# Channel part, first product: seven half products for a pair of row blocks and a pair of hidden tiles, with the prepared weights kept in DRAM

## The chip, the cores and the metric

The kernel runs on one core of a Trainium2 chip. Its engines are PE (matrix products), DVE (vector), ACT (activations), POOL and SP, which issues the DMAs here; each works through its own list in order and waits for the others at semaphores. The metric is the device time of one execution in microseconds (us); less is better. Before the change it is 751.38 us, the median of three runs (751.0 to 753.13).

## What is computed

The attention (local and pooled, 4 x 8 heads, 576 rows of 64) gives `x`, 4 x 576 x 512. Then come a gated layer and a mixing layer, cut to what matters:

```python
h = np.maximum(x @ w_in, 0.0)                       # 512 -> 1024
conv = sum over k of cw[k] * h shifted by k - 1     # three taps along the rows
x = h * sigmoid(conv) @ w_out                       # 1024 -> 512
u = x + (x.T @ U @ V).T                             # rank 32, along the rows
ch = np.maximum(u @ w_ch1, 0.0) @ w_ch2             # 512 -> 2048 -> 512
return u + ch
```

The last two lines are the channel part. The change concerns `u @ w_ch1`.

## The kernel before

The 2304 rows of all four batches are cut into six blocks `g` of 384 rows (`TB`), each of three chunks `c` of 128. Every large product is made of float32 numbers split in two parts, a rounded one ("hi", made by ACT) and the rest ("lo", made by DVE or POOL); three passes (hi by hi, hi by lo, lo by hi) give the product, so each tile of it costs three matmuls.

The order of all work is written out by hand in one long string, `SEQ`. Each of its words names a function and its arguments, and the instructions of each engine stand in the order of these words. A scheduler moves nothing. The string runs through the attention pairs with the unpacking of the weights beside them, through the gated layer (`g1` L647 and `g2` L701), the mixing layer (`mix_in`, `mix_out`) and the channel part, with the stages overlapping.

The weights arrive as 64-bit floats, 512 KB a tile of 128 x 512 (`w_load`). They are unpacked in four steps: one on ACT (L511), three on DVE (L513, L515, L518). Then `w_hi` (ACT, L531) and `w_lo` (POOL or DVE, L534) split them. There are 16 tiles of the gated layer and 32 of the channel part: `w_ch1` at the even, `w_ch2` at the odd places. Before the change all 32 are split once and stay in SBUF.

The channel part runs over the blocks `g` (6) and the hidden tiles `f` of 128 columns (16), that is 96 units `m`:

- `ut_trans` (L759), `ut_hi` (L763), `ut_lo` (L767): per block, four transposed tiles of `u`, split.
- `g3` (L775): 4 chunks of 128 x 3 passes = 12 matmuls of 384 columns into one PSUM bank. Two banks `g` take turns.
- `relu3_hi` (ACT, L780) and `relu3_lo` (DVE, L784): clip and split, straight from the bank into a tile `a` (two tiles take turns).
- `g4` (L793): 3 chunks x 3 passes = 9 matmuls of 512 columns into the three accumulators of the block.
- `flush4` (L801): adds the sum to `u` and writes the rows out, once per chunk.

Of the kernel before, what the change touches and what calls it, by code (L numbers as in the profile page):

```python
# [180 lines left out]

P = 128
NQ, NW = 24, 32
NAW2 = 6
# [711 lines left out]
```

## Time and profile before

| | |
|---|---|
| median of three runs | 751.38 us |
| profiled execution, its own time | 748.79 us |
| its span, first to last instruction | 746.8 us |
| PE busy | 730.4 us, 98% |
| DVE, ACT, POOL busy | 387.8, 295.0, 170.4 us |
| mean granted clock of PE | 0.979 |

The profiled execution lies 2.6 us under the median. An engine's share is an average over stages: the first 100 us are the only stretch in which PE has gaps; from then on it is busy without one. DVE is close to full in the first 120 us and nearly full from 300 to 400 us, where the weights of the channel part are unpacked, and almost idle after that.

### The profile page before, as it was taken

What the parts mean: (1) busy time and instruction counts of PE and PEld (TensorE: products, weight loads), DVE (VectorE), ACT (ScalarE), POOL (GpSimd) and SP (SyncE); (2) the same over time, 40 slices, a digit from 0 to 9 for tenths busy, and PEclk for the clock granted to TensorE, in tenths of its full rate; (3) what the DMA queues carried; (4) which work ended last, traced back from release to release, by engine and by line L of the source; (5) the groups of instructions that cost most, each with busy time, mean ns of one, the idle gap of its engine ahead of it and who ended that gap; (6) DMA issues with size and microseconds to landing.
All of it is one profiled execution on the core that took longest, in us unless ns stands there. A gap on an engine that the chain in (4) does not pass through costs nothing.

```text
span 746.8 us, 15411 instructions
## 1 busy us (share of the span) xinstructions
PE 730.4 (98%) x6655; PEld 651.0 (87%) x6655; DVE 387.8 (52%) x649; ACT 295.0 (39%) x667; POOL 170.4 (23%) x160
## 2 busy tenths in 40 slices
PE   8789999999999999999999999999999999999998
PEld 5578798988888989988998999998989989999887
DVE  6989998867565887889985111311131131112112
ACT  4558676656465856675543111211111111111111
POOL 3765645423233643353330000000000000000000
PEclk9569999999999999999999999999999999999999
DMA  8887523312013000561501000100010010001001
GB/s 243 277 281 240 195 75 90 99 37 72 25 58 113 1 1 29 181 222 51 226 28 43 1 0 1 43 1 0 1 43 1 0 43 1 1 0 43 1 1 42
DMA packets 16387, 52.42 MB, mean 70 GB/s; under 512 B 1984, under 2 KB 2496, under 8 KB 16320
## 3 DMA queue, kind: packets, MB, share of 16 engines
q1 hardware_dynamic: 16320, 51.44, 20.7%
q8 instruction: 52, 0.85, 0.5%
q14 instruction: 15, 0.12, 0.0%
HBM read 46.72 MB, written 4.72 MB: 69 GB/s over the span
## 4 chain that ended last, share of the span: by engine, by line
PE 91%; DMA 5%; DVE 2%; ACT 0%; issue 0%; DVEq 0%; SPq 0%
PE g L775 27%; PE acc L793 26%; PE g L647 14%; PE acc L701 13%; PE O L454 3%; DMA raw<-in_w_dram 2%; PE S L340 1%; DMA vw<-in_vw_dram 1%; PE h L725 1%; PE Sd L393 1%; PE ut L759 1%; PE O L462 1%; PE Td L434 1%; DMA vr<-in_vr_dram 1%; DMA qk<-in_qk_dram 1%; PE mx L746 1%
## 5 line engine op out<-in xcount | busy, mean ns | idle before, releaser
L775 PE MATMUL g<-uT,w 128*128 128x384 f32 x1152 | 213.6, 338 | 0.0
L793 PE MATMUL acc<-w,a 128*128 128x512 f32 x864 | 207.7, 392 | 0.0
L775 PEld LDWEIGHTS g<-uT,w 128*128 128x128 f32 x1152 | 202.3, 188 | 5.1 <-DVE a L784 0.7
L784 DVE SCALAR_TENSOR_TENSOR a<-g,a 128x384 fp32r<-128x384 f32 x96 | 53.4, 556 | 265.7 <-ACT a L780 265.4
L793 PEld LDWEIGHTS acc<-w,a 128*128 128x128 f32 x864 | 161.2, 188 | 31.5 <-issue 0.4
L780 ACT ACTIVATE a<-g 128x384 fp32r<-128x384 f32 x96 | 47.1, 491 | 281.4 <-PE g L775 152.8
L647 PE MATMUL g<-xhl,w 128*128 128x386 f32 (+1 forms) x576 | 117.9, 347 | 0.0
L701 PE MATMUL acc<-w,ghl 128*128 128x512 f32 x432 | 110.0, 396 | 0.0
L647 PEld LDWEIGHTS g<-xhl,w 128*128 128x128 f32 x576 | 102.4, 191 | 5.3 <-issue 1.4
L701 PEld LDWEIGHTS acc<-w,ghl 128*128 128x128 f32 x432 | 79.3, 188 | 14.9 <-issue 0.6
L674 DVE SCALAR_TENSOR_TENSOR g<-h,cw,g 128x384 f32<-128x384 f32 x96 | 59.4, 619 | 22.3 <-ACT g L669 20.5
L534 POOL TENSOR_TENSOR w<-wval,w 128x512 fp32r<-128x512 f32 x34 | 47.5, 1397 | 73.1 <-ACT w L531 71.2
L693 POOL TENSOR_TENSOR ghl<-ct,ghl 128x384 fp32r<-128x384 f32 x40 | 44.0, 1099 | 85.5 <-ACT ghl L690 84.9
L515 DVE SCALAR_TENSOR_TENSOR wval<-raw,wval 128x512 uint32<-128x512 uint32 x48 | 40.5, 846 | 0.9
L531 ACT ACTIVATE w<-wval 128x512 fp32r<-128x512 f32 x48 | 30.0, 628 | 23.3 <-DVE wval L518 23.1
L518 DVE SCALAR_TENSOR_TENSOR wval<-raw,wval 128x512 uint32<-128x512 uint32 x48 | 36.3, 765 | 0.8
L653 ACT ACTIVATE h<-g 128x386 f32<-128x386 f32 (+1 forms) x48 | 23.6, 491 | 27.1 <-PE g L647 26.8
L511 ACT ACTIVATE wval<-raw 128x512 f32<-128x512 f32 x48 | 31.2, 668 | 7.5 <-DMA raw<-in_w_dram 4.1
L454 PEld LDWEIGHTS O<-PT,vw 32*64 32x64 f32 x1536 | 26.3, 144 | 8.8 <-issue 4.7
L454 PE MATMUL O<-PT,vw 32*64 32x24 f32 x1536 | 28.1, 220 | 4.6 <-ACT PT L439 2.3
L678 ACT ACTIVATE g<-g 128x384 f32<-128x384 f32 x48 | 22.7, 474 | 14.6 <-DVE g L674 14.4
L669 ACT ACTIVATE g<-h,cw 128x384 f32<-128x384 f32 x48 | 28.0, 583 | 1.1
(97 smaller groups left out, 639.7 us busy)
## 6 DMA issues: line engine op xcount, KB each, us to landing
raw<-in_w_dram SPq DMA_DIRECT2D x48, 512.0 KB, 4.8
qk<-in_qk_dram SPq DMA_DIRECT2D x16, 576.0 KB, 4.3
vw<-in_vw_dram SPq DMA_DIRECT2D x16, 384.0 KB
vr<-in_vr_dram SPq DMA_DIRECT2D x16, 288.0 KB
out_dram<-u SPq DMA_DIRECT2D x17, 256.0 KB, 2.0
uvr<-in_v_dram SPq DMA_DIRECT2D x1, 576.0 KB
uvr<-in_u_dram SPq DMA_DIRECT2D x1, 320.0 KB
out_dram<-u SPq DMA_DIRECT2D x2, 128.0 KB
```

Of the source, the lines that this page charges most:

```text
L454: nc.tensor.matmul(o[D * h:D * h + D, jh, c:c + NQ], e["vw"][32 * s:32 * s + 32, t, a], e["PT"][32 * s:32 * s + 32, t, 32 * a:32 * a + NQ] ...
L515: nc.vector.scalar_tensor_tensor(out=d, in0=lo, scalar=29, in1=d, op0=ALU.logical_shift_right, op1=ALU.bitwise_or)
L518: nc.vector.scalar_tensor_tensor(out=d, in0=hi, scalar=0x80000000, in1=d, op0=ALU.bitwise_and, op1=ALU.bitwise_or)
L534: eng.tensor_tensor(W[k][:, 1], vals.pop(k), W[k][:, 0].bitcast(F32), op=ALU.subtract)
L647: nc.tensor.matmul(gp[n][:, :wd], w[:, a, cc], xhl[g, cc][:, b, :wd], start=cc == 0 and i == 0, stop=cc == NCC - 1 and i == 2)
L674: nc.vector.scalar_tensor_tensor(out=o, in0=inner(g, hts[n], k), scalar=cw[:, k * NF + f:k * NF + f + 1], in1=o, op0=ALU.mult, op1=ALU.add)
L693: eng.tensor_tensor(ghl[n][:, 1], cts.pop(n), ghl[n][:, 0].bitcast(F32), op=ALU.subtract)
L701: nc.tensor.matmul(acc[g][c], t[:, a, c * P:(c + 1) * P], w[:, b], start=f == 0 and i == 0, stop=f == NF - 1 and i == 2)
L775: nc.tensor.matmul(gp["3", m][:, :TB], w[:, a, cc], uT[g, cc][:, b, :TB], start=cc == 0 and i == 0, stop=cc == NCC - 1 and i == 2)
L780: nc.scalar.activation(out=t[:, 0], in_=gp["3", m][:, :TB], func=AF.Relu)
L784: nc.vector.scalar_tensor_tensor(out=t[:, 1], in0=gp.pop(("3", m))[:, :TB], scalar=0.0, in1=t[:, 0].bitcast(F32), op0=ALU.max, op1=ALU.sub ...
L793: nc.tensor.matmul(acc2[g][c], t[:, a, c * P:(c + 1) * P], w[:, b], start=f == 0 and i == 0, stop=f == NF2 - 1 and i == 2)
```

## The change

`u @ w_ch1` is now computed for a pair of row blocks (`r`, three pairs) and a pair of hidden tiles (`f`, eight pairs) at once. With the 512 columns of `u` cut in two halves, this is a 2 x 2 by 2 x 2 product of half-size pieces, and Strassen's scheme (in Winograd's form) makes it from seven products of sums instead of eight products. A half product is 2 chunks x 3 passes = 6 matmuls, so a unit `q` = (r, f) takes 7 x 6 = 42 matmuls where four units of before, its equal in work, took 48.

What comes with it:

- **Sums of weights.** `s_add` makes four sums of 128 x 256 pieces per `f`; `s_hi`, `s_lo` split the seven factors into tiles `as` (ten in turn, `NAS`). For `r` = 0 they are made, used and written to DRAM (`s_write`, 256 KB each, 56 in all); for `r` = 1 and 2 they are read back (`s_read`, 112 in all). The `w_ch2` tiles stay in SBUF as before, one per pair of places (`w_home`).
- **Sums of u.** Per pair of blocks there are eight groups of three transposes, as before (`u_trans`); then `v_copy` (ACT) and `v_sub` (DVE) make the sums, `b_hi` and `b_lo` split 14 tiles. For `r` = 0 the transposes use the banks `mx0`, `mx1`; for `r` = 1 and 2 they use the two banks of the products.
- **Products.** `product(r, f, j)` runs six matmuls. Products 0, 2, 4, 5 go one on top of the other into the first bank, 1 and then 3, 6 into the second. Between them ACT copies the partial sum out of the first bank (`p_copy`, three per unit) and DVE adds the second bank to such a copy (`p_add`, three per unit). `relu3_hi`, `relu3_lo` and `g4` then work for four results: three from the copies in SBUF, one from the bank.
- **Accumulators.** Two blocks are open at once, so six banks hold them; `mtile` gives three of these to the mixing layer before.
- **The list.** The whole `SEQ` string is new, the attention and the gated layer included. `WAY`, the KB that may be under way behind a load before the next one starts, is 900 instead of 600.

```diff
-    KPB = 3
-    WAY, NLIM = 600, 44
+    KPB, NAS = 3, 10
+    WAY, NLIM = 900, 44
...
+    def s_write(f, j):
+        nc.sync.dma_start(store[f][j], As[0, f, j].rearrange("p a x -> p (a x)").bitcast(F32))
...
+    def v_copy(r, k, i):
+        if i == 0:
+            vb[r, k] = [pools["pm"].tile([P, 2, 512], F32, name="vb", tag="x2a")]
+        nc.scalar.activation(out=vb[r, k][0][:, i, :TB], in_=ut[r, k, i][:, :TB], func=AF.Copy)
...
+    def product(r, f, j):
+        q = r * NFP + f
+        if j in (0, 1, 3):
+            bank[q, int(j > 0)] = gtile(int(j > 0))
+        o = bank[q, int(j in (1, 3, 6))][:, :TB]
+        w = As[r, f, j].rearrange("p a (c j) -> p a c j", c=HC)
+        n = 0
+        for k in range(HC):
+            for a, b in ((0, 0), (0, 1), (1, 0)):
+                nc.tensor.matmul(o, w[:, a, k], Bs[r, j, k][:, b, :TB], start=j in (0, 1, 3) and n == 0, stop=n == 3 * HC - 1, skip_group_check=True)
+                n += 1
+
+    def p_copy(q, i):
+        t = tp[q, i] = ph.tile([P, XW], F32, name="tp", tag="h", bufs=3)
+        nc.scalar.activation(out=t[:, :TB], in_=bank[q, 0][:, :TB], func=AF.Copy)
+
+    def p_add(q, i):
+        t = tp[q, (0, 2, 1)[i]][:, :TB]
+        nc.vector.tensor_tensor(t, bank[q, 1][:, :TB], t, op=ALU.add)
...
-    def g3(m, cc):
...
```

On PE, late in the channel part, where the list of before alternates long runs of `g3` (L775) and `g4` (L793):

```order
L775 MATMUL g<-uT,w 128x384 x15
L793 MATMUL acc<-w,a 128x512 x18
L775 MATMUL g<-uT,w 128x384 x24
L793 MATMUL acc<-w,a 128x512 x18
L775 MATMUL g<-uT,w 128x384 x48
L793 MATMUL acc<-w,a 128x512 x36
```

and the same place now, in unit 18 and at the start of unit 19 (L883 is `product`, L915 `g4`):

```order
L883 MATMUL g<-bt,as 128x384 x6
L915 MATMUL acc<-w,a 128x512 x6
L883 MATMUL g<-bt,as 128x384 x6
L915 MATMUL acc<-w,a 128x512 x3
L883 MATMUL g<-bt,as 128x384 x6
L915 MATMUL acc<-w,a 128x512 x18
L883 MATMUL g<-bt,as 128x384 x18
```

The runs are shorter: one product or a few between groups of `g4`, because each copy out of a bank has to be over before the next product on that bank.

On DVE, in the stage that unpacks the channel weights, before (L513, L515, L518 unpack, L784 is the lower part of the clipped tile, L534 that of a weight):

```order
L784 SCALAR_TENSOR_TENSOR a<-g,a 128x384
L513 TENSOR_SCALAR wval<-wval 128x512
L515 SCALAR_TENSOR_TENSOR wval<-raw,wval 128x512
L518 SCALAR_TENSOR_TENSOR wval<-raw,wval 128x512
L784 SCALAR_TENSOR_TENSOR a<-g,a 128x384
L518 SCALAR_TENSOR_TENSOR wval<-raw,wval 128x512
L534 TENSOR_TENSOR w<-wval,w 128x512 x2
```

and now (L543, L545, L548 unpack; L892 is `p_add`, L903 `relu3_lo`, L805 `s_add`, L821 `s_lo`):

```order
L805 TENSOR_TENSOR sv<-wval 128x256
L892 TENSOR_TENSOR tp<-g,tp 128x384
L548 SCALAR_TENSOR_TENSOR wval<-raw,wval 128x512
L903 SCALAR_TENSOR_TENSOR a<-tp,a 128x384
L903 SCALAR_TENSOR_TENSOR a<-g,a 128x384
L821 TENSOR_TENSOR as<-wval,as 128x256
L892 TENSOR_TENSOR tp<-g,tp 128x384
L821 TENSOR_TENSOR as<-wval,as 128x256
L821 TENSOR_TENSOR as<-sv,as 128x256 x4
```

Additions that PE waits for (L892, L903) now stand among the unpacking and the splitting of the sums.

On PE, where the transposes of the last rows of `u` stand, before:

```order
L775 MATMUL g<-uT,w 128x384 x24
L759 MATMUL ut<-ident,u_4779 128x128 x6
L793 MATMUL acc<-w,a 128x512 x18
L775 MATMUL g<-uT,w 128x384 x3
L759 MATMUL ut<-ident,u_4779 128x128 x3
L775 MATMUL g<-uT,w 128x384 x45
```

and now, between the second and the third pair of blocks (L836 transposes):

```order
L836 MATMUL g<-ident,u_4494 128x128 x3
L836 MATMUL g<-ident,u_4889 128x128 x3
L915 MATMUL acc<-w,a 128x512 x6
L836 MATMUL g<-ident,u_4889 128x128 x3
L915 MATMUL acc<-w,a 128x512 x9
L836 MATMUL g<-ident,u_4494 128x128 x6
L836 MATMUL g<-ident,u_4889 128x128 x6
L915 MATMUL acc<-w,a 128x512 x3
L836 MATMUL g<-ident,u_4494 128x128 x3
L915 MATMUL acc<-w,a 128x512 x6
L883 MATMUL g<-bt,as 128x384 x30
```

All eight groups of transposes of a pair now stand together, in the banks that the products use, with 24 matmuls of `g4` among them and no product.

## Rows read from the trace of the kernel before

**Rows 1.** Page: busy time, share, instructions; the span in 40 slices, tenths busy.

```profile
PE 730.4 (98%) x6655; PEld 651.0 (87%) x6655; DVE 387.8 (52%) x649; ACT 295.0 (39%) x667; POOL 170.4 (23%) x160
...
PE   8789999999999999999999999999999999999998
...
DVE  6989998867565887889985111311131131112112
...
PEclk9569999999999999999999999999999999999999
```

**Rows 2.** Chain of work that ended last: start us, us, engine, tile, line, matmuls.

```profile
660.00 8.16 PE acc L793 x36
...
726.52 8.39 PE g L775 x48
```

**Rows 3.** Groups by line and form: busy us, mean ns, idle before and its releaser.

```profile
L775 PE MATMUL g<-uT,w 128*128 128x384 f32 x1152 | 213.6, 338 | 0.0
L793 PE MATMUL acc<-w,a 128*128 128x512 f32 x864 | 207.7, 392 | 0.0
...
L784 DVE SCALAR_TENSOR_TENSOR a<-g,a 128x384 fp32r<-128x384 f32 x96 | 53.4, 556 | 265.7 <-ACT a L780 265.4
L780 ACT ACTIVATE a<-g 128x384 fp32r<-128x384 f32 x96 | 47.1, 491 | 281.4 <-PE g L775 152.8 <-PE acc L793 128.5
...
L801 DVE TENSOR_TENSOR u<-u,acc 128x256 f32<-128x256 f32 x2 | 0.8, 418 | 0.0
```

**Rows 4.** Timeline at 592 us, one tight handoff: start, us, engine, line; [idle before].

```profile
592.10 3.58 PE L793 MATMUL acc<-w,a 128*128 128x512 f32 x15
594.36 0.49 ACT L780 ACTIVATE a<-g 128x384 fp32r<-128x384 f32 x1 [5.76 <-PE acc L793]
594.88 0.56 DVE L784 SCALAR_TENSOR_TENSOR a<-g,a 128x384 fp32r<-128x384 f32 x1 [5.70 <-ACT a L780]
595.49 2.06 PEld L775 LDWEIGHTS g<-uT,w 128*128 128x128 f32 x12 [0.24 <-DVE a L784]
595.52 2.36 PE L775 MATMUL g<-uT,w 128*128 128x384 f32 x12
```

**Rows 5.** Windows of 20 us: PE, PEld, DVE, ACT, POOL busy, clock, DMA share, GB/s.

```profile
340.00:360.00 20.00, 20.00 (x101) 17.92 (x100) 18.40 (x33) 9.27 (x17) 4.98 (x4) 1.00 0.08 27
360.00:380.00 20.00, 20.00 (x108) 17.98 (x107) 17.86 (x32) 11.78 (x22) 7.57 (x7) 1.00 0.62 237
```

**Rows 6.** DVE and POOL from 340 to 400 us by line and form, columns as in rows 3.

```profile
L515 DVE SCALAR_TENSOR_TENSOR wval<-raw,wval 128x512 uint32<-128x512 uint32 x19 | 14.3, 758 | 0.5
L518 DVE SCALAR_TENSOR_TENSOR wval<-raw,wval 128x512 uint32<-128x512 uint32 x20 | 13.7, 695 | 0.4
L513 DVE TENSOR_SCALAR wval<-wval 128x512 uint32<-128x512 uint32 x19 | 8.7, 466 | 0.2 <-ACT wval L511 0.2
...
L534 POOL TENSOR_TENSOR w<-wval,w 128x512 fp32r<-128x512 f32 x13 | 18.3, 1410 | 42.3 <-ACT w L531 42.3
```

**Rows 7.** Single lines over the span: min/median/max ns, first and last start.

```profile
L513 DVE TENSOR_SCALAR wval<-wval x48: 411/420/1519, 18.3 to 395.3; 128x512 uint32<-128x512 uint32 x48
...
L515 DVE SCALAR_TENSOR_TENSOR wval<-raw,wval x48: 644/692/2355, 19.5 to 395.8; 128x512 uint32<-128x512 uint32 x48
...
L534 POOL TENSOR_TENSOR w<-wval,w x34: 1254/1298/1765, 22.8 to 398.0; 128x512 fp32r<-128x512 f32 x34
...
L420 POOL TENSOR_TENSOR vd<-vr x12: 721/736/1054, 8.3 to 212.9; 72x256 f32<-72x256 f32 x12
```

**Rows 8.** Timeline at 337 us, a POOL instruction and the DVE instruction beside it.

```profile
337.43 1.30 POOL L716 TENSOR_TENSOR x<-u,x 128x512 fp32r<-128x512 f32 x1 [0.67 <-ACT x L712]
...
337.53 1.74 DVE L515 SCALAR_TENSOR_TENSOR wval<-raw,wval 128x512 uint32<-128x512 uint32 x1
```

**Rows 9.** DMA issues of the whole span, KB each, median us from issue to landing.

```profile
raw<-in_w_dram SPq DMA_DIRECT2D x48, 512.0 KB, 4.8
...
out_dram<-u SPq DMA_DIRECT2D x17, 256.0 KB, 2.0
```

More of the change, by code (lines that the diff above doesn't have):

```diff
@@ L215, in mixer_kernel @@
     pv = ctx.enter_context(tc.tile_pool(name="pv", bufs=3, side="right", reuse_waits="tile"))
-    ph = tc.alloc_tile_pool(name="ph", bufs=1, side="right", reuse_waits="tile")
+    ph = ctx.enter_context(tc.tile_pool(name="ph", bufs=1, side="right", reuse_waits="tile"))
+    pe = ctx.enter_context(tc.tile_pool(name="pe", bufs=1, side="right", reuse_waits="tile"))
     px = tc.alloc_tile_pool(name="px", bufs=1, side="right", reuse_waits="tile")
-    pe = tc.alloc_tile_pool(name="pe", bufs=1, side="right", reuse_waits="tile")
+    dram = ctx.enter_context(tc.tile_pool(name="dram", bufs=1, space=bass.MemoryType.DRAM))
     pa = tc.alloc_tile_pool(name="pa", bufs=1, reuse_waits="tile")
@@ L491, in w_home @@
         g, i = k
[L492 to L494 removed]
+        return wp, f"w{i if g == 1 else i // 2}"
     def w_load(*k):
@@ L722, in mix_in @@
         if j == 4 * odd:
-            hps[b] = pools["psb"].tile([P, DM], F32, name="h1", tag="hh")
+            hps[b] = mtile(2, "h1")
         for a in range(2):
@@ L738, in mix_out @@
     def mix_out(pair, j):
-        p = mx[pair, j] = pools["psb"].tile([P, DM], F32, name="mx", tag="mx", bufs=2)
+        p = mx[pair, j] = mtile((pair * KPB * NCH + j) % 2, "mx")
         mm = []
@@ L751, in mix_add, with half @@
         nc.vector.tensor_tensor(u, u, mx.pop((pair, j)), op=ALU.add)
-    uT, acc2, a_, ut = {}, {}, {}, {}
-    def ut_trans(g, cc):
-        p = ut[g, cc] = pools["psb"].tile([P, 512], F32, name="ut", tag="mx", bufs=2)
+    NFP = NF2 // 2
+    As, Bs, vb, ut, a_, acc2, sv, tp, bank = {}, {}, {}, {}, {}, {}, {}, {}, {}
+    HC = NCC // 2
+    store = [[dram.tile([P, 512], F32, name=f"s{f}_{j}") for j in range(7)] for f in range(NFP)]
+    def half(i, k):
+        return vals[2, i][:, 256 * k:256 * k + 256]
@@ new lines, in s_add, with s_src @@
+    def s_add(eng, f, i):
+        w, x = 4 * f, 4 * f + 2
+        if i == 0:
+            sv[f] = pools["wa"].tile([P, 4, 256], F32, name="sv", tag="sv")
+            a, b = half(x, 0), half(x, 1)
+        elif i == 1:
+            a, b = sv[f][:, 0], half(w, 0)
+        elif i == 2:
+            a, b = half(w, 0), half(x, 0)
+        else:
+            a, b = half(w, 1), sv[f][:, 1]
+        eng.tensor_tensor(sv[f][:, i], a, b, op=ALU.subtract if i else ALU.add)
+    def s_src(f, j):
+        if j < 2 or j == 5:
+            return half(4 * f + 2 * (j == 5), int(j > 0))
+        return sv[f][:, {2: 1, 3: 0, 4: 2, 6: 3}[j]]
@@ new lines, in s_tile, with s_hi, s_lo, s_read @@
+    def s_tile():
+        return pools["wa"].tile([P, 2, 256], F32R, name="as", tag="as", bufs=NAS)
+    def s_hi(f, j):
+        As[0, f, j] = s_tile()
+        nc.scalar.activation(out=As[0, f, j][:, 0], in_=s_src(f, j), func=AF.Copy)
+    def s_lo(eng, f, j):
+        t = As[0, f, j]
+        eng.tensor_tensor(t[:, 1], s_src(f, j), t[:, 0].bitcast(F32), op=ALU.subtract)
+    def s_write(f, j):
+        nc.sync.dma_start(store[f][j], As[0, f, j].rearrange("p a x -> p (a x)").bitcast(F32))
+    def s_read(r, f, j):
+        t = As[r, f, j] = s_tile()
+        nc.sync.dma_start(t.rearrange("p a x -> p (a x)").bitcast(F32), store[f][j])
@@ L758, in ut_trans, with u_trans @@
+    def u_trans(r, i):
+        k, i = divmod(i, 4)
+        g, cc = ((2 * r, k), (2 * r + 1, k), (2 * r + 1, k + HC), (2 * r, k + HC))[i]
+        p = ut[r, k, i] = (mtile if r == 0 else gtile_named)(i % 2, "ut")
         for c in range(NCH):
             nc.tensor.transpose(p[:, c * P:(c + 1) * P], U_[g][:, c, cc * P:(cc + 1) * P], ident)
-    def ut_hi(g, cc):
-        t = uT[g, cc] = xt.tile([P, 2, XW], F32R, name="uT", tag="xt")
-        nc.scalar.activation(out=t[:, 0, :TB], in_=ut[g, cc][:, :TB], func=AF.Copy)
@@ L765, in ut_lo @@
-    def ut_lo(g, cc):
-        t = uT[g, cc]
-        nc.vector.tensor_tensor(t[:, 1, :TB], ut.pop((g, cc))[:, :TB], t[:, 0, :TB].bitcast(F32), op=ALU.subtract)
-    def g3(m, cc):
-        g, f = divmod(m, NF2)
-        if cc == 0:
-            gp["3", m] = gtile()
-        w = W[2, 2 * f].rearrange("p a (c j) -> p a c j", c=NCC)
-        for i, (a, b) in enumerate(((0, 0), (0, 1), (1, 0))):
-            nc.tensor.matmul(gp["3", m][:, :TB], w[:, a, cc], uT[g, cc][:, b, :TB],
-                             start=cc == 0 and i == 0, stop=cc == NCC - 1 and i == 2)
@@ L778, in relu3_hi, with gtile_named @@
-    def relu3_hi(m):
-        t = a_[m] = p1.tile([P, 2, TB], F32R, name="a", tag="ga")
-        nc.scalar.activation(out=t[:, 0], in_=gp["3", m][:, :TB], func=AF.Relu)
-    def relu3_lo(m):
-        t = a_[m]
-        nc.vector.scalar_tensor_tensor(out=t[:, 1], in0=gp.pop(("3", m))[:, :TB], scalar=0.0, in1=t[:, 0].bitcast(F32),
-                                       op0=ALU.max, op1=ALU.subtract)
-    def g4(m, c):
-        g, f = divmod(m, NF2)
-        if f == 0:
-            acc2.setdefault(g, {})[c] = pools["psg"].tile([P, DM], F32, name="acc", tag=f"acc{c}")
-        t, w = a_[m], W[2, 2 * f + 1]
+    def gtile_named(k, name):
+        return gtile(k)
@@ new lines, in v_copy, with v_sub @@
+    def v_copy(r, k, i):
+        if i == 0:
+            vb[r, k] = [pools["pm"].tile([P, 2, 512], F32, name="vb", tag="x2a")]
+        nc.scalar.activation(out=vb[r, k][0][:, i, :TB], in_=ut[r, k, i][:, :TB], func=AF.Copy)
+    def v_sub(r, k, i):
+        if i == 1:
+            vb[r, k].append(pools["pm"].tile([P, 2, 512], F32, name="vb", tag="x2b"))
+        (a, s), (b, o) = (((0, 0), (0, 0)), ((0, 0), (1, 0)), ((0, 1), (0, 1)), ((1, 0), (1, 1)))[i]
+        nc.vector.tensor_tensor(vb[r, k][b][:, o, :TB], ut[r, k, (1, 2, 2, 3)[i]][:, :TB], vb[r, k][a][:, s, :TB], op=ALU.subtract)
@@ new lines, in b_src, with b_hi @@
+    def b_src(r, k, j):
+        if j in (0, 1, 6):
+            return ut[r, k, {0: 0, 1: 3, 6: 2}[j]][:, :TB]
+        a, s = {2: (1, 0), 3: (0, 0), 4: (0, 1), 5: (1, 1)}[j]
+        return vb[r, k][a][:, s, :TB]
+    def b_hi(r, k, j):
+        i = 2 * j + k
+        if i < 6:
+            t = pools["pb"].tile([P, 2, TB], F32R, name="bt", tag=f"b{i}")
+        elif i == 6:
+            t = pools["wa"].tile([P, 2, TB], F32R, name="bt", tag="b6")
+        else:
+            t = xt.tile([P, 2, XW], F32R, name="bt", tag="xt")
+        Bs[r, j, k] = t
+        nc.scalar.activation(out=t[:, 0, :TB], in_=b_src(r, k, j), func=AF.Copy)
@@ new lines, in p_copy, with r_src, relu3_hi @@
+    def p_copy(q, i):
[4 more added lines that the diff above has]
+        nc.vector.tensor_tensor(t, bank[q, 1][:, :TB], t, op=ALU.add)
+    def r_src(q, k):
+        return bank[q, 0][:, :TB] if k == 3 else tp[q, (0, 2, 1)[k]][:, :TB]
+    def relu3_hi(q, k):
+        t = a_[q, k] = p1.tile([P, 2, TB], F32R, name="a", tag="ga")
+        nc.scalar.activation(out=t[:, 0], in_=r_src(q, k), func=AF.Relu)
@@ new lines, in relu3_lo, with g4 @@
+    def relu3_lo(q, k):
+        t = a_[q, k]
+        nc.vector.scalar_tensor_tensor(out=t[:, 1], in0=r_src(q, k), scalar=0.0, in1=t[:, 0].bitcast(F32),
+                                       op0=ALU.max, op1=ALU.subtract)
+    def g4(q, n, c):
+        k, blk, fo = ((0, 0, 0), (1, 1, 1), (3, 0, 1), (2, 1, 0))[n]
+        r, f = divmod(q, NFP)
+        g = 2 * r + blk
+        if f == 0 and n < 2:
+            acc2.setdefault(g, {})[c] = mtile(c, "acc") if blk else pools["psg"].tile([P, DM], F32, name="acc", tag=f"acc{c}")
+        t, w = a_[q, k], W[2, 2 * (2 * f + fo) + 1]
@@ L792, in g4 @@
         for i, (a, b) in enumerate(((0, 0), (0, 1), (1, 0))):
             nc.tensor.matmul(acc2[g][c], t[:, a, c * P:(c + 1) * P], w[:, b],
-                             start=f == 0 and i == 0, stop=f == NF2 - 1 and i == 2)
+                             start=f == 0 and n < 2 and i == 0, stop=f == NFP - 1 and n >= 2 and i == 2)
     def flush4(g, c):
@@ L825, in mixer_kernel @@
         "mi": mix_in, "mH": mix_h, "mo": mix_out, "ma": mix_add,
-        "u": ut_trans, "uT": ut_hi, "uL": ut_lo, "3": g3, "r3": relu3_hi, "R3": relu3_lo, "4": g4, "o": flush4,
+        "sa": lambda *k: s_add(GP, *k), "sA": lambda *k: s_add(DV, *k), "sh": s_hi, "sl": lambda *k: s_lo(DV, *k),
+        "sL": lambda *k: s_lo(GP, *k), "sw": s_write, "sr": s_read, "u": u_trans, "bv": v_copy, "bt": v_sub, "bh": b_hi,
+        "bl": lambda *k: b_lo(DV, *k), "bL": lambda *k: b_lo(GP, *k), "p": product, "pc": p_copy, "pa": p_add,
+        "rh": relu3_hi, "rl": relu3_lo, "4": g4, "o": flush4,
     }
```

30 lines of the change are left out of this document (14 added, 16 removed), and 354 rows, old and new, of the table SEQ.

## The prediction, made before the changed kernel was run

> **What bounds the kernel now.** I read the page first. PE is busy for 98% of the span, in its row of 40 slices only the first three and the last are under nine tenths, and its granted clock is down in the second and third alone [rows 1]. So the kernel is bound by the number and width of its matmuls, and anything that leaves matmuls out is worth their whole time, as long as PE finds its operands ready. What a matmul costs is read from the chain, where long runs stand in order of time: 48 of `g3` take 8.39 us, 0.175 us each, and 36 of `g4` take 8.16 us, 0.227 us each [rows 2]. (The means of 338 and 392 ns [rows 3] overlap and aren't used.) Short runs cost no more than long ones there. Then I read DVE, since what the change adds lies there: it is 92% and 89% busy in the two windows in which the weights are unpacked, and PE is full in both all the same [rows 5].
>
> **What is removed.** A pair of blocks and of hidden tiles takes 42 matmuls instead of 48, in 24 units: 144 matmuls fewer. 144 x 0.175 = 25.2 us off PE, all of it from the stretch in which PE is full. `g4` keeps its 864, the transposes their number.
>
> **The copies and additions between products.** Each of the 24 units adds three copies (ACT) and three additions (DVE) of 128 x 384, 0.49 and 0.56 us each by the nearest rows, `relu3_hi` and `relu3_lo` [rows 3]. After the first pair of blocks ACT and DVE have little else to do: 7 such ACT instructions are 3.4 us, 7 DVE ones 3.9 us, beside a unit of 42 x 0.175 + 36 x 0.227 = 15.5 us. It is not their sum that counts but whether each ends in time. For that I take one tight handoff of before apart [rows 4]: the run of 15 starts at 592.10, so its ninth matmul, which frees the tile `a`, ends near 592.10 + 9 x 0.227 = 594.14. ACT starts at 594.36, 0.22 later; DVE ends at 595.44; PE loads weights again at 595.49. So ACT and DVE together need about 1.35 us, one of them alone 0.22 + 0.49 (0.56) + 0.05 = 0.76 (0.83). There, six matmuls of `g4`, 1.36 us, lay in between, and PE lost some 0.02 us. In the new list I counted the matmuls in each gap. Where one copy or addition has to be over there is at least one product, 6 x 0.175 = 1.05 us (once, in the first unit, 0.69, short by 0.14). Where clip and split have to be over there are at least six matmuls of `g4`, again 1.36 us, eight times. So these handoffs cost nearly nothing, 0.14 + 8 x 0.02 = 0.3 us. If the cover were short by as little as 0.2 us at all six in a unit, that would be 24 x 6 x 0.2 = 29 us, the whole gain.
>
> **The change from one pair of blocks to the next.** Before, transposes lay between long runs in banks of their own. Now, for the second and third pair, eight groups share two banks with nothing but `g4` among them. I walked through both places with 0.49 (ACT), 0.56 (DVE) and the handoff above. At the first, with 33 matmuls of `g4`, DVE has 19 instructions, 10.6 us, beside PE's 11.1; PE waits some 0.5 us. At the second, with 24, four groups of transposes stand in a row, each behind a bank that DVE has to free: PE waits 0.9 + 0.7 + 0.2 + 0.1 = 1.9 us. Together 2.4; I take 2.5, bounds 0.5 (covers as good as before) and 6 (each of 16 groups late by 0.4).
>
> **The first pair of blocks, where everything comes together.** Between the first product and the transposes of the second pair the new list has, on PE, 56 products, 85 groups of `g4` and the rest of the layers before: 59 + 58 + 6 = 123 us. In it DVE has 85 unpacking steps (28 tiles at 0.42 + 0.69 + 0.69 = 1.80 us, by the medians of L513 and L515 [rows 7] and the mean of L518 [rows 6]: 51), 23 additions and 30 splits at 0.56 (30), 42 short instructions of 128 x 256 (the nearest row has 0.42 [rows 3]: 18) and some 8 us more: 107. POOL has 37 short ones at about 0.74 (its nearest row is 72 x 256 [rows 7]), 7 of 128 x 512 at 1.30 and 5 others: 27 + 9 + 6 = 42. The two get in each other's way: a DVE step of 0.69 took 1.74 beside a POOL instruction [rows 8]. From 340 to 400 us the means of L515 and L513 [rows 6] lie over their medians [rows 7] by 19 x 0.066 + 19 x 0.046 = 2.1 us in all, while POOL worked for 18.3, so about 0.12 us of DVE per us of POOL. That makes DVE 107 + 0.12 x 42 = 112 us of 123, 91%. In one window of before it was 92% and PE didn't wait [rows 5]; now it stays there for 120 us, six times as long, with additions that PE waits for standing among the steps. I allow 2 us of waiting for this, bounds 0 and 12 (ten per cent of the stage).
>
> The Trainium skill says more ("SBUF — State Buffer", Who interferes with whom): a DVE instruction with two inputs in SBUF and a POOL instruction that reads SBUF shut each other out for the whole instruction. The trace agrees where the two meet (1.74 against 0.69 us), not that they always meet; if all of POOL's time fell on DVE, the stage would be short by 26 us, and that is the second rival.
>
> **Weights through DRAM.** 56 writes of 256 KB; the nearest row is the output's, 2.0 us to land [rows 9]. A tile `as` is filled again ten tiles later; from a write's place in the list to that there are at least 5.9 us of matmuls. 112 reads of 256 KB: between 2.0 and the 4.8 us of a 512 KB load [rows 9]; from the product that frees a tile to the one that uses it again there are at least 9.4 us. The stage moves some 28 MB in 123 us, 230 GB/s; DMA moved 237 GB/s at 62% in one window [rows 5]. So I cost it at nothing; if a load landed 3 us late once per unit, ACT would stop in front of its unpacking step with the copies queued behind it, 8 x 2 = 16 us.
>
> **The rest.** The new list also reorders the attention and lets 900 KB be under way. DVE is nearly full in the first 120 us in both lists and has about 2 us more to do by then, loads can only fill gaps of DMA; I take 0, bounds -3 and +3. At the end two blocks are flushed in place of one, but the last one still waits for a single addition and a write: 0, bounds 0 and +1.
>
> **Sum.** Against the profiled execution: 748.8 - 25.2 + 0.3 + 2.5 + 2 = 728.4. The median lies 2.6 above it: 731.0.
>
> **The rivals.**
> 1. *DVE sets the pace of the first pair of blocks* (the second bound above): its 91% is an average, and units with more splitting on POOL go over. For it: DVE and POOL stand closer than anywhere before; against: 0.12, not 1, is what the trace shows. A third of POOL's time blocking DVE gives 107 + 14 = 121 of 123, and in a list worked through in order perhaps 12 us of waiting: 741.
> 2. *All of POOL's time blocks DVE*: 107 + 42 = 149, 26 us over PE's 123. 731.0 - 2 + 26 = 755.
> 3. *Each addition comes late* (ends slower): in the first pair of blocks 53 instructions of DVE that PE waits for (23 additions, 30 splits) may each find DVE in a blocked step of 1.74 instead of 0.69, 1.05 later, and the covers above have nothing to spare. From 22 / 53 = 0.42 us each on, the kernel is slower than before by over 0.3%; at 0.6 it is 731.0 - 2 + 32 = 761. Against: the same steps stood ahead of `relu3_lo` before, with PE full.
> 4. *The product is no shorter*: groups of six matmuls with a wait each, on a bank that was just read, lose 0.15 us at each of 168 starts, 25 us: 751 + 5 = 756. Against: weights are loaded ahead, and after a restart of 0.24 us PE went on within 0.03 us [rows 4].
>
> **Chances.** About 0.3% (2.3 us) is what a measurement of this kernel can tell from no change. Forecast (723 to 737) 0.68; first rival (737 to 748) 0.19; second 0.03; third 0.06; fourth 0.04. The slow ends of the rivals and a little of the first one's give same 0.04, slower 0.09; faster 0.87. The range has to leave out no more than 0.2: 723 (the lower bounds together: 2 + 2 + 3 us less) to 743, inside the first rival.
>
> **What would show it.** PE's busy time falls by about 25 us, with 0.175 us per matmul in L883; its gaps after 100 us are two short ones at the changes of block pairs (by my count of PE's work near 455 and 590 us) and small ones between 335 and 455. DVE is over 90% busy there and under 30% later. If PE waits for L892 or L903 throughout, the third rival holds; if for L821 or L543 to L548 in the first pair alone, the first. A clock below 1.0 after 100 us, or reads that land later than 9 us, would break the sum in a way that I haven't priced.

## The result, and the profile after

| | before | after |
|---|---|---|
| median (runs) | 751.19 us (4: 749.03 to 753.13) | 740.27 us (4: 738.63 to 744.0) |
| ratio, 95% interval | | 0.9862 (0.9816 to 0.9909) |
| profiled execution, its span | 748.79, 746.8 | 739.66, 737.5 |

The change makes the kernel 10.9 us faster. The forecast was 20.4 (751.4 to 731.0): the sign was right and the range holds the time, but the time lies 9.3 us above the forecast. The page of the changed kernel, the lines that answer to [rows 1]:

```profile
PE 712.7 (97%) x6516; PEld 629.9 (85%) x6516; DVE 459.1 (62%) x792; ACT 352.9 (48%) x807; POOL 202.3 (27%) x205
...
PE   7778999999999999999999999999999989999997
...
DVE  6699889885647546869989998842221264222223
...
PEclk9658999999999999999999999999999999999999
```

PE is busy for 17.7 us less, not 25, though the work left out is there: the timeline of PE in the changed kernel, in the middle of the second pair of blocks (L883 is the half product, L915 is `g4`; start, us, line, number of matmuls):

```profile
520.45 1.21 PE L883 MATMUL g<-bt,as 128*128 128x384 f32 x6
521.50 2.89 PE L915 MATMUL acc<-w,a 128*128 128x512 f32 x12
524.23 1.21 PE L883 MATMUL g<-bt,as 128*128 128x384 f32 x6
525.28 1.53 PE L915 MATMUL acc<-w,a 128*128 128x512 f32 x6
526.65 2.27 PE L883 MATMUL g<-bt,as 128*128 128x384 f32 x12
528.76 0.86 PE L915 MATMUL acc<-w,a 128*128 128x512 f32 x3
```

From start to start, six matmuls of a half product take 1.05 us and twelve 2.11: 0.175 each, as in [rows 2], and nothing stands between the runs. So a busy share can't tell where the time went, since a matmul that starts late or runs at half clock is busy too. I worked out PE's lost time instead: the time elapsed, less every matmul begun by then times the median distance from such a matmul to the next one at full clock (such a matmul followed by one of its kind, over all kernels of this study: 0.176 us for 384 columns, 0.227 for 512, 0.007 to 0.2 for the attention's). It comes from the traces, one profiled execution for each kernel:

```
us lost by    60    130    260    340    400    480    600    640    end
before      32.4   45.6   58.2   58.4   58.7   58.9   59.4   59.6   63.8
after       34.2   52.1   66.8   68.0   69.5   71.1   71.5   74.3   79.2
```

PE's work fell from 746.8 - 63.8 = 683.0 to 737.5 - 79.2 = 658.3 us: 24.7, the 25.2 of the forecast less five more filler matmuls in the new list (26, before 21; 6655 - 6516 = 139 = 144 - 5, so the trace lacks none). The lost time grew by 15.4, of which the forecast had 4.8. **8.6 of it stand ahead of 260 us, where not one product of the new kind runs.** The windows that show them, of before and then of after (PE, PEld, DVE, ACT, POOL busy, clock, DMA share, GB/s):

```profile
60.00:130.00 70.00, 68.77 (x1296) 60.03 (x1295) 64.39 (x109) 51.54 (x135) 35.62 (x33) 1.00 0.45 145
```

```profile
60.00:130.00 70.00, 65.99 (x1268) 57.37 (x1269) 63.82 (x103) 48.12 (x127) 32.42 (x30) 0.95 0.39 130
```

In these 70 us PE stands idle 2.8 us longer and runs at the lower of its two clock levels, 1.2 GHz, for 70 x 0.05 x 2 = 7 us, where before it was at 2.4 all the time. PE's waits of after in the timeline there, in brackets with what ended them:

```profile
70.64 1.01 PE L327 MATMUL O<-mask,identR 128*128 128x224 f32 x7 [1.85 <-DVE X L513]
...
91.86 1.57 PE L425 MATMUL Sd<-ss,qd 128*96 128x144 f32 x6 [1.52 <-ACT PT L471]
```

Before had one of 0.9 us in these 70. The granted clock is 0.83 in the 10 us around the end of either of the two, at 70 to 80 and 90 to 100 us, and 1.00 in the 10 us between: the lower level came with each wait. The other profiled executions bear that out: from 60 to 130 us ten of the kernels of this study have 15 waits of 1.5 us or more on PE, and at each of them the clock falls, during the wait or within 1.5 us of its end; no single wait of 0.8 to 1.0 us there is followed by a fall. L327 at 70.64 is seven filler matmuls of the list, which compute nothing.

### The profile page after: what moved, and what is told of

Read it like the earlier page. It is cut to its first block, busy times and chain, and to the rows that moved or that the text cites. A ratio compares the mean times of both kernels' runs of the same rounds, so it can differ in the third digit from the quotient of the medians.

```text
span 737.5 us, 16004 instructions
## 1 busy us (share of the span) xinstructions
PE 712.7 (97%) x6516; PEld 629.9 (85%) x6516; DVE 459.1 (62%) x792; ACT 352.9 (48%) x807; POOL 202.3 (27%) x205
## 4 chain that ended last, share of the span: by engine, by line
PE 87%; DVE 7%; ACT 2%; issue 2%; DMA 1%; POOL 1%; DVEq 0%; ACTq 0%; POOLq 0%
PE acc L915 25%; PE g L883 23%; PE g L677 13%; PE acc L731 13%; PE O L486 3%; PE Sd L425 1%; PE O L494 1%; PE S L372 1%; DVE wval L545 1%; PE Td L466 1%; DMA vr<-in_vr_dram 1%; PE h L755 1%; PE T L459 1%; PE spin L312 1%; DVE bt L872 1%
## 5 line engine op out<-in xcount | busy, mean ns | idle before, releaser
L915 PE MATMUL acc<-w,a 128*128 128x512 f32 x864 | 214.6, 392 | 0.0
L883 PE MATMUL g<-bt,as 128*128 128x384 f32 x1008 | 193.2, 337 | 0.6 <-DVE tp L892 0.4
L883 PEld LDWEIGHTS g<-bt,as 128*128 128x128 f32 x1008 | 178.7, 188 | 10.4 <-DVE tp L892 1.8
L915 PEld LDWEIGHTS acc<-w,a 128*128 128x128 f32 x864 | 160.4, 188 | 27.3
L892 DVE TENSOR_TENSOR tp<-g,tp 128x384 f32<-128x384 f32 x72 | 40.0, 555 | 91.4 <-ACT tp L888 51.9
L731 PEld LDWEIGHTS acc<-w,ghl 128*128 128x128 f32 x432 | 79.6, 189 | 15.2 <-issue 0.6
L888 ACT ACTIVATE tp<-g 128x384 f32<-128x384 f32 x72 | 35.2, 489 | 100.8 <-PE g L883 100.7
L903 DVE SCALAR_TENSOR_TENSOR a<-tp,a 128x384 fp32r<-128x384 f32 x72 | 40.8, 568 | 64.4 <-ACT a L899 64.2
L899 ACT ACTIVATE a<-tp 128x384 fp32r<-128x384 f32 x72 | 37.8, 525 | 87.4 <-PE acc L915 46.9
L872 POOL TENSOR_TENSOR bt<-vb,bt 128x384 fp32r<-128x384 f32 x12 | 13.1, 1097 | 132.5 <-ACT bt L868 132.4
L564 POOL TENSOR_TENSOR w<-wval,w 128x512 fp32r<-128x512 f32 x24 | 31.5, 1315 | 60.7 <-ACT w L561 53.4
L545 DVE SCALAR_TENSOR_TENSOR wval<-raw,wval 128x512 uint32<-128x512 uint32 x48 | 42.9, 893 | 1.1
L548 DVE SCALAR_TENSOR_TENSOR wval<-raw,wval 128x512 uint32<-128x512 uint32 x48 | 36.2, 756 | 0.8
```

The lines of the kernel that those rows point to most:

```text
L545: nc.vector.scalar_tensor_tensor(out=d, in0=lo, scalar=29, in1=d, op0=ALU.logical_shift_right, op1=ALU.bitwise_or)
L548: nc.vector.scalar_tensor_tensor(out=d, in0=hi, scalar=0x80000000, in1=d, op0=ALU.bitwise_and, op1=ALU.bitwise_or)
L731: nc.tensor.matmul(acc[g][c], t[:, a, c * P:(c + 1) * P], w[:, b], start=f == 0 and i == 0, stop=f == NF - 1 and i == 2)
L883: nc.tensor.matmul(o, w[:, a, k], Bs[r, j, k][:, b, :TB], start=j in (0, 1, 3) and n == 0, stop=n == 3 * HC - 1, skip_group_check=True)
L892: nc.vector.tensor_tensor(t, bank[q, 1][:, :TB], t, op=ALU.add)
L899: nc.scalar.activation(out=t[:, 0], in_=r_src(q, k), func=AF.Relu)
```

## The experiments

Five facts hold for all that follow: each was compared with runs of the kernel before on the same chip (medians 750.96 to 751.06 us); the changed kernel, "after", was not run again beside them, so a difference from its 740.27 is good to a few us only, and the ratios with their intervals decide; line numbers shift by one or two with an edit; "words" are the entries of `SEQ`; and where the start of one list is followed by another, what stands behind it is every word of the other list that isn't done yet, in its order (without its fillers).

### `rev`: the kernel before, with the start of the new list

```diff
-    WAY, NLIM = 600, 44
+    WAY, NLIM = 900, 44
-SEQ = (list of before)
+SEQ = (list of after up to the word 2.21.2, then the rest of the list of before)
```

> The kernel before, with the attention and gated layer up to about 200 us in the order of the new list and 900 KB under way; the products of before. Theory A: 751.2 + 8 = 759. Theory C: 751.

759.29 us (4 runs, 757.84 to 760.68), ratio 1.01 (1.0067 to 1.0132): 8.3 us slower than before. Lost time is 66.7 at 260 us (after: 66.8) and grows by 5.5 from there to the end, as in before (5.6). So the new start of the list costs 8 us by itself (5 to 10 by the interval), with the old product behind it. With the order `rev` takes over the new list's fillers, the engine that it gives to some of the steps, and the limit of 900; of these only the limit (`way600`) and the fillers (`nofill`) were tried alone.

### `way600`: the changed kernel with the old limit for loads

```diff
-    WAY, NLIM = 900, 44
+    WAY, NLIM = 600, 44
```

> The changed kernel with 600 KB under way in place of 900, nothing else. Theory A (the order of the new list's first 130 us costs some 8 us): still 740, within 1.5. Theory B (the deeper queue of loads does it, as a load that is waited for lands behind others): 733 to 736. Theory C (the products, their copies and the DVE of the first pair of blocks cost it): 740.

743.66 us (8 runs, 740.45 to 749.3), ratio 0.9899 (0.9868 to 0.993). Nothing is won back; the limit isn't the cause. It is 3.4 us more than after, outside what theories A and C allowed, though the intervals of the two ratios overlap. The kernels that follow with an old start have the limit of 600 too and none of the fillers of `nofill`; so `way600` is the nearer one to compare them with.

### `front216`, `front500`, `front900`: the changed kernel with the first words of the list from before

```diff
-    WAY, NLIM = 900, 44
+    WAY, NLIM = 600, 44
-SEQ = (list of after)
+SEQ = (first N words of the list of before, then the rest of the list of after)
```

> The changed kernel, but the first 216 words of its list (up to the opening of the products, some 52 us) in the order of before, with 600 KB under way; the words after that in the new order. Theory A: if the loss lies ahead of the first product of the gated layer, 733; if it lies behind, in the interplay of attention and gated layer from 60 to 110 us, 738 to 740. Theory C: 740.

> The changed kernel with the first 900 words of its list (the attention and most of the gated layer beside it, some 190 us) in the order of before, with 600 KB under way; the words after that in the new order, Strassen's products untouched. Theory A: 740.3 - 8 = 732, and the granted clock full after 60 us. Theory C: 739 to 741, since all that it blames is still there.

> The changed kernel with only the first 500 words of the list taken from the kernel before (the first 130 us or so), its planner number of 600, and none of the new list's fillers behind them. Theory A: the loss is that of the words that run from 60 to 130 us, where lost TensorE time grows from +1.8 to +6.9 us against before, so 740.3 less 5 to 7: 733 to 735. Theory B: any join of the two lists costs what it saves, as the join behind 900 words did (from 130 to 260 us it lost 16.2 us where before lost 10.6): 737 to 741.

- N = 216, up to about 55 us: 740.93 (737.74 to 742.3), ratio 0.985 (0.9811 to 0.9889). No gain over after (2.7 us below `way600`, within the intervals), so most of the loss lies behind the attention's beginning. Lost time at 60 us is 34.6, at 130 it is 54.5. None of the fillers of `nofill` stand here, but PE waits 1.8 and 1.5 us at 67.8 and 95.7 us for other work, and the clock falls at both.
- N = 900: 736.77, the median of four runs (733.45 to 737.8), ratio 0.9786 (0.9744 to 0.9827). A fifth execution, the profiled one, took 2384 us, stretched over its whole length (some 140 matmuls in 100 us of the channel part where after has 500), and isn't used. 3.5 us below after is about half of what theory A expected, and the intervals of the two ratios just overlap; 6.9 below `way600` is most of it.
- N = 500: 739.4 (737.39 to 741.32), ratio 0.9835 (0.9809 to 0.986), which is theory B. At 100 us the lost time is 44.8, 4.4 less than in after, but at 130 the two are level again, at 52.1.

What happened with 500 words stands in PE's waits of that kernel from 60 to 130 us (total, times, longest):

```profile
PE T L460 <- POOL P L419: 3.9, 1, 3.9
PE Sd L426 <- ACT Pd L438: 1.0, 1, 1.0
PE T L460 <- ACT Pd L438: 0.9, 1, 0.9
```

and in one of its windows:

```profile
100.00:120.00 20.00, 16.11 (x264) 14.40 (x263) 17.44 (x30) 14.08 (x40) 8.76 (x8) 0.92 0.18 61
```

The wait of 3.9 at 116.8 us is where the two lists join: the transposes `T` stand there in the order of the new list, behind probabilities `P` that POOL, in the order of the old one, hasn't made yet. Whoever changes half of such a list pays at the seam.

### `nofill`: the changed kernel without two groups of fillers

```diff
-... r1.1 f.7 2.0.0 ...
+... r1.1 2.0.0 ...
-... gL.2 f.5 Td.7.0 ...
+... gL.2 Td.7.0 ...
```

> The changed kernel without two words of its list that issue filler matmuls behind the first 60 us: seven of them at 70.6 us, which waited 1.85 us for the copy of the attention output that reads the bank they write, and five at 93.4 us. Theory A: what the new list lost behind 60 us is partly the fillers' own doing, their wait (1.85) and their length (0.9 and 0.6, the rows of L327 at 70.64 and 93.35), so about 3 us go and the time is 737 (740.3 less 3.3); with them goes the half clock of 3.4 us that follows the wait at 70.6 in the trace, about 1.5 more. Theory B: the work behind the fillers is not ready any earlier, the wait moves to the next matmul and the engine stands idle where it ran fillers: 740 within 1 us. Rival C: without them the clock falls for longer than now (half-clock time over the 38 us of the profiled run), and the time goes above 742.

738.14 us (736.46 to 740.64), ratio 0.9835 (0.9809 to 0.986). The intervals of this ratio and of after's overlap, so the 2.1 us are likely rather than certain; they lie between theory A (3) and B (0). The trace bears out half of the mechanism. The waits of this kernel from 60 to 260 us:

```profile
PE Sd L426 <- ACT PT L472: 1.6, 1, 1.6
PE S L366 <- DVE X L514: 0.8, 1, 0.8
PE acc L732 <- ACT ghl L721: 0.5, 1, 0.5
PE Td L467 <- DVE X L514: 0.4, 1, 0.4
PE Td L467 <- DVE sm L414: 0.3, 1, 0.3
PE S L366 <- DVE P L395: 0.2, 1, 0.2
PE T L460 <- POOL Pd L443: 0.2, 1, 0.2
```

and its windows of the place:

```profile
60.00:80.00 20.00, 18.24 (x471) 15.15 (x470) 19.37 (x30) 15.05 (x43) 11.21 (x10) 1.00 0.35 112
60.00:130.00 70.00, 65.95 (x1272) 56.77 (x1271) 66.04 (x106) 50.07 (x133) 34.69 (x32) 0.97 0.40 134
```

The wait of 1.85 us is gone and the clock doesn't fall there (1.00, after had 0.91 in this window). But 2.0 us of shorter waits came in its place (0.8, 0.5, 0.4 and 0.3), behind the same copy `X` in part, and PE is idle in these 70 us for as long as in after (busy for 65.95, after 65.99): the wait moved, as theory B had it. What was won is the time that the fillers themselves took on PE, and the lower clock behind one of the two waits (0.97, after 0.95). The fillers had been put where the bank that they write was still being read.

### `best900` and `front1012`: longer starts from before

The same edit: `best900` is N = 900 with the stores of `flush_late` (below), `front1012` is N = 1012 alone, up to about 240 us.

> The changed kernel with the first 900 words of the list taken from the kernel before and its planner number of 600, and the output stores of flush_late. Theory A: the loss in the first 130 us is that of the list alone (8.7 us of lost TensorE time at 260 us against before), and the new product's gain stands behind it: 740.3 less 4 to 8 less 2, so 730 to 734. Theory B: the old list's start only moves the loss behind the place where the two lists join, as the 736 to 737 of the kernel with the same first 900 words let one think: 736 to 738. Its profile tells where: lost TensorE time at 130 us near 46 us (as before) and what is added between 130 and 360 us.

> The same with the first 1012 words from the kernel before, so that the two lists join behind the attention of the pairs 8 to 11 and the waits seen at 203 to 208 us (0.6, 0.7 and 1.0 us, with a half clock of 3.4 us behind them) are not met. Theory A: what is left of the front's loss goes with them: 736.7 less 3 to 5, so 732 to 734. Theory B: the join's price moves along with it: 736 to 738.

`best900`: 736.66 (735.96 to 738.63), ratio 0.9817 (0.9794 to 0.9839). **`front1012`: 733.97 (732.9 to 735.48), ratio 0.9764 (0.9744 to 0.9784), the fastest kernel of the study**, 6.3 us below the changed one, and clear of it by the intervals (`best900` isn't). Lost time of the kernels with an old start, to be read beside the table of before and after:

```
us lost by    60    130    260    340    400    480    600    640    end
front500    33.5   52.1   66.7   67.8   69.4   71.0   71.4   75.8   80.5
best900     34.3   46.6   65.2   66.4   68.4   69.7   70.5   72.7   77.4
front1012   33.9   47.0   62.2   63.5   64.9   66.4   69.5   69.7   74.4
```

Up to 130 us both are within 1.4 of before. `best900` then loses 18.6 up to 260, where before loses 12.6: its seam is at 203 to 208 us. Its waits on PE from 60 to 260 us include

```profile
PE T L461 <- POOL P L420: 1.0, 1, 1.0
...
PE O L488 <- ACT PTd L478: 0.7, 1, 0.7
PE Sd L427 <- ACT PT L473: 0.6, 1, 0.6
```

and the clock is 0.99 over the 130 us. `front1012` has one such wait left (1.0 us at 237 us), and the clock stays at 1.00. It is faster than both kernels with the old attention joined to the new product, at a place where the seam costs little: from 130 to 260 us it loses 15.2, before 12.6.

### `flush_late`: output stores behind the next pair's sums

```diff
-... bh.1.0.3 o.0.0 ... rl.8.0 ...
+... bh.1.0.3 ... rl.8.0 o.0.0 ...
```

and `o.2.0` to `o.2.2`, `o.3.0` to `o.3.2` likewise, to places around `rl.16.0` and `rl.16.1`.

> The changed kernel with the output stores of the blocks o.0.0, o.2 and o.3 later in the list, behind the first sums of the next pair of blocks; nothing else. Theory A (the block-pair changes cost what the walk gave, because the sums bt and the transposes stand on VectorE behind the evictions of the finished blocks): the 1.86 us of idle time at 600 to 620 us, and what the losses there show (2.9 us from 600 to 640), shrink, so 738.3 (740.3 less 2). Theory B (the waits there come from ScalarE's transpose copies or from the product's own length, not from the evictions): no change, 740.3 within 1 us.

740.55 (737.76 to 744.57), ratio 0.9868 (0.9829 to 0.9907): theory B. Lost time from 600 to 640 us is 2.4, after 2.8. The evictions on DVE aren't most of what PE waits for; with them gone 1.3 of the 1.9 us of waiting are left, nearly in one piece. PE's waits from 598 to 612 us in after, and from 598 to 616 in `flush_late`:

```profile
PE g L836 <- DVE bt L872: 1.0, 2, 0.6
PE g L836 <- DVE vb L851: 0.8, 2, 0.6
```

```profile
PE g L837 <- DVE bt L873: 1.1, 1, 1.1
PE g L837 <- DVE vb L852: 0.2, 1, 0.2
```

### `dec_twice`: 22 us more for DVE in the first pair of blocks

```diff
-        dec(raws[k], vals[k], step)
+        for _ in range(2 if k[0] == 2 and step == 3 else 1):
+            dec(raws[k], vals[k], step)
```

> The changed kernel with the last unpacking step of every channel weight done twice on VectorE (the same operation again on the same tile, so that the values stay), 28 more operations of 0.69 to 0.75 us in the first pair of blocks. It asks whether the first pair of blocks was at VectorE's limit, as the prediction's term of 2 us and its first rival took it. VectorE was busy 91% there (17.1 to 18.7 of each 20 us, TensorE 20.0 of 20), about 112 of 123 us; 20 us more make 131 of 123. Theory A (the limit is where the sum of busy times puts it): +8 us at least, 748 to 752. Theory B (slack ahead of it and work that can move to other stretches take most of it): under +4 us, 740 to 744.

(The line ran 80 times, 48 in after: 32 more, 29 of them from 340 us on; 32 x 0.69 = 22.1 us.) 760.56 us (756.93 to 762.73), ratio 1.0126 (1.0094 to 1.0158): 20.3 us slower than after. Theory A, and more than its 8: by these medians all but some 2 us of the added work landed in the time. The runs of either kernel lie 5 to 6 us apart, so the 2 is rough; in the profiled executions the lost time behind 260 us grew by some 19 us, which says the same. Windows of after and then of `dec_twice` over the same stretch:

```profile
340.00:480.00 140.00, 138.89 (x696) 123.28 (x695) 125.51 (x223) 83.84 (x180) 53.14 (x55) 1.00 0.63 217
```

```profile
340.00:480.00 140.00, 127.28 (x606) 107.56 (x605) 132.44 (x221) 73.39 (x160) 53.09 (x53) 1.00 0.55 193
```

DVE's busy time only goes from 125.5 to 132.4 of 140, 95%, then PE stops; 4.3 of the 7.6 us in which DVE is still idle it waits for ACT. So the 90% that it had here in after were close to full. The waits on PE from 340 to 480 us in `dec_twice` say on what:

```profile
PE g L885 <- DVE tp L894: 8.4, 10, 3.0
PE g L885 <- DVE ct L717: 1.5, 1, 1.5
PE g L885 <- ACT tp L890: 1.3, 1, 1.3
PE acc L917 <- DVE a L905: 1.1, 2, 0.8
```

The additions `tp` (L892 of after) come late because they stand among the unpacking steps; that is the way the forecast's first rival would have gone. (By the signs that the forecast gave, a wait for L892 pointed at the third rival. With DVE full in this stage alone the two look the same there.)

### `split_pool`: all low halves of the sums on POOL

```diff
-... sl.F.J ...      (32 words: s_lo on DVE)
+... sL.F.J ...      (s_lo on POOL)
```

> The changed kernel with all 56 low halves of the sums of weights on GpSimd, where 32 of them stood on VectorE: VectorE is rid of 32 operations of 0.42 to 0.56 us (13 to 18 us of its 109 in the 120 us of the first pair of blocks), GpSimd has 32 more of 0.74 to 0.92 us (27 us, 47 to 74 of 120). Theory A (GpSimd's work stands beside VectorE's): VectorE falls to under 80% busy there, its operations keep their lengths, and the time falls by the 1 to 2 us that the stage loses now: 738 to 739.5. Theory B, the second rival (GpSimd's time blocks VectorE's): VectorE's operations there grow by what it was rid of or more, 13 to 27 us; its busy share stays and the time is 740 or more, up to 752. Where GpSimd itself becomes late, waits on its halves would show.

747.58 (744.33 to 748.04), ratio 0.9934 (0.9908 to 0.9961): the time of theory B, at the mild end. It is 7 us slower than after by the medians, 5 by the ratios, whose intervals just touch. DVE was rid of 13 to 18 us and its busy time from 340 to 480 us fell by 11 (125.5 to 114.5), where theory B had it stay. The groups of DVE from 340 to 460 us (count, busy us, mean ns), of after and then of `split_pool`:

```profile
L543 DVE TENSOR_SCALAR wval<-wval 128x512 uint32<-128x512 uint32 x28 | 14.4, 514 | 1.8 <-ACT wval L541 1.6
L903 DVE SCALAR_TENSOR_TENSOR a<-tp,a 128x384 fp32r<-128x384 f32 x21 | 12.4, 592 | 2.3 <-ACT a L899 2.1
L903 DVE SCALAR_TENSOR_TENSOR a<-g,a 128x384 fp32r<-128x384 f32 x7 | 3.9, 554 | 2.0 <-ACT a L899 2.0
```

```profile
L544 DVE TENSOR_SCALAR wval<-wval 128x512 uint32<-128x512 uint32 x26 | 16.1, 620 | 8.5 <-ACT wval L542 8.5
L904 DVE SCALAR_TENSOR_TENSOR a<-tp,a 128x384 fp32r<-128x384 f32 x21 | 15.1, 727 | 4.7 <-ACT a L900 4.6
L904 DVE SCALAR_TENSOR_TENSOR a<-g,a 128x384 fp32r<-128x384 f32 x7 | 3.9, 553 | 2.7 <-ACT a L900 2.7
```

With 47 to 68 us of POOL in these 120, the split from two SBUF tiles (`a<-tp,a`) went from 592 to 727 ns and the unpacking step from 514 to 620. The same split with one operand in a PSUM bank (`a<-g,a`) stayed at 553. So POOL's work does lengthen DVE's, where DVE reads SBUF alone, and only by part of POOL's time. The Trainium skill ("SBUF — State Buffer", Who interferes with whom) says that a DVE instruction with at most one SBUF input, outside DVE's two-port modes, stays clear of POOL, and one with two SBUF inputs doesn't when POOL reads SBUF. The trace agrees for the two forms of the split (553 and 727 ns). L543 has one input and grew too; whether it ran in such a mode no run here shows.

That isn't all that made the kernel slower, since DVE had time left. ACT waited longer for the sums `sv` that POOL makes, in after and then in `split_pool` from 340 to 460 us:

```profile
ACT as L817 <- POOL sv L805: 2.5, 5, 1.4
ACT as L818 <- POOL sv L806: 7.2, 10, 2.1
```

DVE in turn waited longer for ACT (ahead of the unpacking step L543 8.5 us, in after 1.6), and PE for the additions on DVE (3.4 us, in after 0.4). So POOL was also late itself. Which of the two, the longer steps on DVE or the late sums, costs how much, this run doesn't part.

### `copy_twice`: each copy between half products twice

```diff
-        nc.scalar.activation(out=t[:, :TB], in_=bank[q, 0][:, :TB], func=AF.Copy)
+        for _ in range(2):
+            nc.scalar.activation(out=t[:, :TB], in_=bank[q, 0][:, :TB], func=AF.Copy)
```

> The changed kernel with each of the product's copies on ScalarE (tp from the bank, 72 of them at 0.489 us) done twice, which makes the way from a half product to the word that uses its bank again 0.49 us longer each time. Rival 3 (each addition late): if half products wait for these copies and additions, each longer copy shows: 72 of 0.49 us, 35 us at most, and 10 or more in any case: over 750. Theory A (the cover of a product of other half products and outputs is longer than copy and addition together in all but the 15 places with a cover of 1.05 us): 3 to 5 us at most, 740 to 745.

747.67 (10 runs, 742.88 to 750.94), ratio 0.9951 (0.9927 to 0.9976): 7.4 us slower, between the two theories. Of the 72 x 0.49 = 35 us added, a fifth shows. Lost time grows by 7.0 from 340 to 480 us (after: 3.1), by 1.7 from 480 to 600 (0.4) and by 3.8 from 600 to 640 (2.8). The covers hold most of a longer copy, but the margin is thinner than I had it.

## Why the prediction was right in sign, and 9 us short

**The terms of the sum, by lost time of after less that of before.**

| step of the prediction | forecast | measured |
|---|---|---|
| products left out | -25.2 | -24.7 |
| copies and additions in between | +0.3 | -0.1 (480 to 600 us) |
| changes of block pairs | +2.5 (0.5 to 6) | +4.0 (400 to 480, 600 to 640 us) |
| first pair of blocks | +2 (0 to 12) | +1.2 (340 to 400 us) |
| the new list up to 260 us ("the rest") | 0 (-3 to +3) | **+8.6** |
| 260 to 340 us | 0 | +1.0 |
| the end (640 us on) | 0 (0 to +1) | +0.7 |
| sum | -20.4 | -9.3 |

748.8 - 9.3 = 739.5, and the profiled execution took 739.66. (The medians give 10.9 in place of 9.1: the profiled execution of before lies 2.4 us under its median, that of after 0.6.)

- **That the range holds 740.3 is luck.** The time lies in the stretch that the forecast gave to the first rival, and the range reached that far for its sake. Its mechanism cost 1.2 us; the time got there by a term that the forecast had bounded at 3.
- **The step that failed is "The rest".** I let the new order of the attention and the gated layer go at 0 with bounds of 3, arguing from DVE's and the loads' shares there. The order itself was at hand, and shares say nothing of the order in which PE meets what it waits for. `rev` shows that this start costs 8.3 us alone. Of the 8.6 in the table, 4.7 are lost from 60 to 130 us, where the two waits and the clock behind them stand; `nofill` took the fillers and the clock behind one of the two away and likely won about 2 us; and `front1012`, which puts the old start back, wins 6.3. Why the start of the list was changed at all can't be read from these runs. The remaining 1.8 us up to 60 us and 2.1 from 130 to 260 weren't split further.
- **The products** did what they were costed at, so rival 4 falls: no loss at the starts of groups of six (0.175 us a matmul in the timeline above).
- **The changes of block pairs.** PE's idle time is 0.55 us at the first and 1.86 at the second, the 0.5 and 1.9 of the walk. But PE lost 1.4 and 2.6. The timeline of after shows the rest:

```profile
603.14 0.52 PE L836 MATMUL g<-ident,u 128*128 128x128 f32 x3 [0.63 <-DVE vb L851]
604.27 0.52 PE L836 MATMUL g<-ident,u 128*128 128x128 f32 x3 [0.61 <-DVE bt L872]
605.21 0.55 PE L836 MATMUL g<-ident,u 128*128 128x128 f32 x3 [0.43 <-DVE bt L872]
605.52 0.94 PE L915 MATMUL acc<-w,a 128*128 128x512 f32 x3
```

  Three transposes are 3 x 0.11 = 0.33 us when others follow, but 0.52 when a wait comes next: the tail of the last one isn't covered. So the idle time in brackets is less than the loss. Which instruction on ACT or DVE is the one to move there stays open; `flush_late` shows that the evictions are 0.4 us of it at most.
- **The first pair of blocks** cost 1.2 of the 2, and DVE was busy 108.7 of 120 us, 91% as worked out. Rival 1's time, 741, is what came, but not by its mechanism: PE was busy 20.00 of 20 us in every window from 360 to 460 us. `dec_twice` shows how near it was, with some 2 us to spare, as far as these runs can tell, where I read 9% of 123 as 11.
- **Rival 2** (POOL blocks DVE): right in kind, wrong in size. L543, L545, L548, L903 and L821 together took 10.6 us more than their medians from 340 to 460 us, beside 46.6 us of POOL: 0.23 of POOL's time. The forecast had 0.12, the rival 1. In `split_pool`, with 68 us of POOL, the same steps grew further, and POOL's own lateness came on top.
- **Rival 3** (each addition late) falls: in after one such wait of 0.4 us is left (`tp`, at 355 us), and `copy_twice` shows 0.10 us lost for each 0.49 of delay. (The forecast's 0.42 us each would give 731.0 - 2 + 22 = 751, the time of before, and not yet 0.3% more.)
- **Weights through DRAM** cost nothing. Reads landed within the bounds. The weight tiles took 5.9 us where 4.8 was assumed, and the writes 4.9 where the nearest row had 2.0, still under the 5.9 to the next filling (KB, median us to landing; [rows 9]). PE waited for none of them:

```profile
as<-s SPq DMA_DIRECT2D x112, 256.0 KB, 2.7
raw<-in_w_dram SPq DMA_DIRECT2D x48, 512.0 KB, 5.9
s<-as SPq DMA_DIRECT2D x56, 256.0 KB, 4.9
```
